# Zero tile and banks first, closer clock-keeping products, an earlier flag and a new order in a fused attention and MLP kernel

## The chip, the cores and the metric

The kernel runs on one core of a Trainium2 chip. Its engines work in parallel, each through its own list of instructions: TensorE (PE, with weight loads as PEld), VectorE (DVE), ScalarE (ACT), GpSimd (POOL) and SyncE (SP, which issues most of the transfers). They wait for each other by semaphores. The metric is the device time of one execution in microseconds (us), from the first instruction to the last and with a little around it; lower is better.

## The reference

The program computes a linear attention with a decaying state and puts its output through a two-layer MLP whose gate is a cosine. r, k, v, w and u are of 4 bytes, w_in and w_out of 8 bytes (the kernel reads each of their numbers as a pair of words).

```
for t in range(S):                       # S = 768, B = 4, H = 8, D = 48
    cur   = (u * k_t) outer v_t
    y_t   = r_t @ (state + cur)
    state = w * state + k_t outer v_t
x = y as (B*S, H*D)                      # 3072 x 384
h = x @ w_in                             # 384 x 2048
out = (h * cos(h)) @ w_out               # 2048 x 384
```

## The kernel before

The 3072 tokens are cut into 24 chunks of 128. A chunk of the attention is computed in matrix form: k and r are multiplied by tables of powers of the decay w (`decT_k`, `decT_r`, `dec_k`, built once at the start from w by a transpose, line 539, and VectorE, lines 544 to 564), then scores (`mm_a`, line 1072, or `mm_az`, 1211 and 1219), a mask, and the output transposed (`mm_x`, line 1110 or 1268), which becomes x as a high and a low part, `xh` and `xl` (lines 1281 and 1286). The first six chunks take an own "early" way with transposes on TensorE (line 946); the others come "late", with VectorE's transposes. Each weight tile is loaded raw, converted by ScalarE, VectorE and GpSimd, and split into a high and a low part (`conv`, lines 740 to 787).

Three chunks make a block of 384 tokens. A step is one block and one slice of 128 hidden columns: nine products of 384 columns give h (line 376), then ScalarE and VectorE in turn make the whole turns (388), the rest (391), the cosine (394), the gate (1390) and its two parts gh and gl (1393, 1396), and nine products of 384 columns (line 383) add to three accumulators. There are 128 steps; the last two work in pieces of 128 columns. Results are copied (1423, 1425) and stored (1435 to 1439).

All this is written as about 2345 operations, each with its engine, a due time, a cost, what it needs, and its buffers. `Plan.order` (line 243 on) goes through a table of numbers, PLACE, which holds each operation's rank: on each engine the operation of lowest rank is next, and the planner works out a start for it from the costs. The program is then emitted in the order of those starts. So PLACE sets each engine's list, and the planned starts set two more things: which buffer an operation gets, and how many clock-keeping products stand in a gap of TensorE. These are products of a tile of zeros, `warm`, into an unused part of bank 2 of the accumulators (`warm_up`, line 1452). They add zero and depend on nothing but the zero tile and on what was read last from that part of the bank; they are there so that TensorE has work in a gap. `start_banks` (line 527) is a group of six products of 512 columns of the same zeros, which sets banks 2 to 7 once.

At the start VectorE clears `warm` (line 496, `start_dve`), the pads of the buffers (line 501, `start_pads`) and a row (508); GpSimd makes the identity; SyncE loads w, then k, r and u. At the end stands a second way through the whole program, for inputs out of range: `check_range` looks at the weights again, `flag_set` at w, `fine_min` takes a minimum over the checks (691 to 693), `fine_t` transposes it (696), `flag_all` writes the flag (699, 700), and each engine then loads the flag from memory (line 1467) and branches (line 1468) over the general path. With ordinary inputs that path is not taken.

Of the kernel before, what the change touches and what calls it, by code (L numbers as in the profile page):

```python
# [154 lines left out]
WARM_TO = 75.0  # L155
# [146 lines left out]
def kernel(  # L302
# [11 lines left out]
    nc = tc.nc  # L314
# [5 lines left out]
    P = 128  # L320
# [76 lines left out]
    with ExitStack() as actx:  # L397
# [107 lines left out]
        def wr():  # L505
# [3 lines left out]
        o_pool = op(POOL, -99, 1.0, start_pool)  # L509
        o_pool2 = op(POOL, -98, 2.75, start_pool2)  # L510
        o_dve = op(DVE, -99, 0.2, start_dve)
        o_pads = op(DVE, -98, 2.3, start_pads)

        o_w = op(
            SP,
# [936 lines left out]
        def warm_up(n):  # L1452
            for _ in range(n):
                nc.tensor.matmul(psum[:, 2, DM : DM + P], warm, warm, start=o_banks not in made, stop=True, skip_group_check=True)
# [150 lines left out]
```

## Time and profile before

| | |
|---|---|
| median of 3 runs | 515.59 us (514.53 to 515.60) |
| profiled execution | 516.15 us, its span 514.4 us |
| TensorE busy | 489.1 us, 95% |
| VectorE busy | 390.8 us, 76% |
| ScalarE, GpSimd busy | 304.4 us, 59%; 198.9 us, 39% |
| mean granted clock of TensorE | 0.985 |
| moved by DMA | 60.92 MB, 118 GB/s over the span |

A busy TensorE is not TensorE at its peak: the ends of pipelined matmuls are modelled, and a product of 384 columns that is listed with 340 ns starts 0.175 us after the one before it when nothing is in the way. The clock is a share of 2.4 GHz; 0.5 is its lower level, 1.2 GHz. A wait is named by the operation that ended it.

### The profile page before, as it was taken

The page shows a single profiled execution, that of the slowest core. Times are in us where ns is not written, and L with a number is a line of the kernel's source. Part 1 is how long each engine was busy: PE and PEld are TensorE (multiplying, and loading weights), DVE is VectorE, ACT ScalarE, POOL GpSimd, SP SyncE. Part 2 cuts the span into 40 slices and gives each one's busy share as a digit, 9 for nine tenths or more (in the row PEclk, how much of TensorE's full clock was granted, in tenths as well). Part 3 has the DMA queues.
Part 4 walks back from the last instruction along what each step waited for, and adds up shares of the span by engine and source line. Part 5 has one row for each costly group of instructions (what it writes and reads, how often), then busy time and mean ns, then how long its engine had stood idle before and what let it go on. Part 6 is the DMA issues. An engine that isn't in the chain of part 4 may idle for free.

```text
span 514.4 us, 13429 instructions
## 1 busy us (share of the span) xinstructions
PE 489.1 (95%) x5207; PEld 464.4 (90%) x5207; DVE 390.8 (76%) x813; ACT 304.4 (59%) x775; POOL 198.9 (39%) x198
## 2 busy tenths in 40 slices
PE   6788899999999999999999999999999999999993
PEld 4667799999898998899999999999999999999992
DVE  6888899998999888967777987885575556564652
ACT  1767587885766655565565665656354565454351
POOL 6846445556597767543171442813110020000000
PEclk9978999999999999999999999999999999999997
DMA  7985558868878778573472557643352222010001
GB/s 137 196 177 122 153 168 195 190 173 171 152 149 154 161 140 171 127 171 117 103 180 65 124 148 156 170 84 100 76 138 63 61 59 81 1 48 0 2 0 53
DMA packets 140086, 60.92 MB, mean 118 GB/s; under 512 B 118205, under 2 KB 135870, under 8 KB 140014
## 3 DMA queue, kind: packets, MB, share of 16 engines
q1 hardware_dynamic: 137070, 55.86, 46.1%
q0 software_dynamic: 2656, 3.74, 4.9%
q8 instruction: 42, 0.69, 0.6%
q10 hardware_dynamic: 288, 0.39, 0.2%
q14 instruction: 30, 0.25, 0.1%
HBM read 51.31 MB, written 8.26 MB: 116 GB/s over the span
## 4 chain that ended last, share of the span: by engine, by line
PE 65%; DVE 6%; ACT 1%; DMA 1%; issue 1%; SPq 0%; POOL 0%; DVEq 0%; ACTq 0%
PE psum L376 29%; PE psum L383 29%; PE psum L1268 3%; PE psum L1211 2%; PE psum L1219 1%; DVE gl L1396 1%; DMA raw<-in_r_dram 1%; DVE psum L1390 1%; DVE T L1238 1%; DVE f L391 1%; DVE psum L1253 0%; ACT gh L1393 0%; DVE T L960 0%; ACT qi L388 0%; ACT f L394 0%
## 5 line engine op out<-in xcount | busy, mean ns | idle before, releaser
L383 PE MATMUL psum<-w_out_hi,gh 128*128 128x384 f32 x384 | 133.4, 347 | 2.7 <-ACT gh L1393 2.0
L376 PE MATMUL psum<-xh,w_in_hi 128*128 128x384 f32 x384 | 130.4, 340 | 1.9 <-DVE gl L1396 1.9
L383 PE MATMUL psum<-w_out_hi,gl 128*128 128x384 f32 x384 | 131.0, 341 | 0.6 <-DVE gl L1396 0.6
L383 PE MATMUL psum<-w_out_lo,gh 128*128 128x384 f32 x384 | 130.0, 339 | 0.0
L376 PE MATMUL psum<-xl,w_in_hi 128*128 128x384 f32 x384 | 129.1, 336 | 0.5 <-DVE xl L1286 0.3
L376 PE MATMUL psum<-xh,w_in_lo 128*128 128x384 f32 x384 | 129.3, 337 | 0.0
L1396 DVE TENSOR_TENSOR gl<-psum,gh 128x384 fp32r<-128x384 f32 (+1 forms) x132 | 71.2, 539 | 46.1 <-ACT gh L1393 44.2
L394 ACT ACTIVATE f<-f 128x384 f32<-128x384 f32 (+1 forms) x132 | 67.4, 514 | 51.2 <-DVE f L391 49.2
L388 ACT ACTIVATE qi<-psum 128x384 int32<-128x384 f32 (+1 forms) x132 | 63.2, 480 | 55.6 <-PE psum L376 50.4
L1393 ACT CAST gh<-psum 128x384 fp32r<-128x384 f32 (+1 forms) x132 | 61.6, 468 | 57.4 <-PE psum L383 34.5
L1390 DVE TENSOR_TENSOR psum<-psum,f 128x384 f32<-128x384 f32 (+1 forms) x132 | 72.0, 548 | 24.7 <-ACT f L394 22.8
L391 DVE SCALAR_TENSOR_TENSOR f<-psum,qi 128x384 f32<-128x384 f32 (+1 forms) x132 | 70.7, 537 | 23.8 <-ACT qi L388 23.0
L1190 POOL TENSOR_TENSOR T<-T,k 48x512 f32<-48x512 f32 x36 | 47.2, 1311 | 99.9 <-issue 35.4
L383 PEld LDWEIGHTS psum<-w_out_hi,gh 128*128 128x128 f32 x384 | 72.5, 189 | 6.6 <-ACT gh L1393 2.8
L376 PEld LDWEIGHTS psum<-xh,w_in_hi 128*128 128x128 f32 x384 | 72.1, 188 | 4.6 <-DVE gl L1396 3.4
L383 PEld LDWEIGHTS psum<-w_out_hi,gl 128*128 128x128 f32 x384 | 72.6, 189 | 2.5 <-DVE gl L1396 2.0
L376 PEld LDWEIGHTS psum<-xl,w_in_hi 128*128 128x128 f32 x384 | 72.2, 188 | 1.1 <-DVE xl L1286 1.1
L383 PEld LDWEIGHTS psum<-w_out_lo,gh 128*128 128x128 f32 x384 | 72.4, 189 | 0.0
L376 PEld LDWEIGHTS psum<-xh,w_in_lo 128*128 128x128 f32 x384 | 72.1, 188 | 0.0
L770 POOL TENSOR_TENSOR f<-f,raw 128x384 int32<-128x384 int32 x32 | 35.0, 1094 | 46.2 <-DVE f L759 20.1
L1176 ACT ACTIVATE T<-ident,a 128x128 f32<-128x128 f32 x144 | 47.1, 394 | 2.8 <-DVE a L1032 2.7
L974 POOL TENSOR_TENSOR f<-f,f 128x384 f32<-128x384 f32 x18 | 18.8, 1047 | 38.8 <-DMA f<-in_r_dram 32.1
(146 smaller groups left out, 633.0 us busy)
## 6 DMA issues: line engine op xcount, KB each, us to landing
raw<-in_moe_w_out_dram SPq DMA_DIRECT2D x32, 384.0 KB, 3.7
raw<-in_moe_w_in_dram SPq DMA_DIRECT2D x32, 192.0 KB, 3.9
raw<-in_moe_w_in_dram SPq DMA_DIRECT2D x16, 384.0 KB, 3.7
raw<-in_k_dram SPq DMA_DIRECT2D x71, 80.0 KB, 3.1
raw<-in_r_dram SPq DMA_DIRECT2D x71, 80.0 KB, 2.6
out_dram<-f SPq DMA_DIRECT2D x21, 192.0 KB, 2.5
out_dram<-f POOLq DMA_DIRECT2D x19, 192.0 KB, 4.8
f<-in_k_dram SPq DMA_DIRECT2D x18, 192.0 KB, 3.7
```

The lines of the kernel that those rows point to most:

```text
L376: nc.tensor.matmul(ph, a, b_, start=(i == 0), stop=(i == len(mm) - 1))
L383: nc.tensor.matmul(acc, a[:, ts], b_, start=(first and i == 0), stop=(last and i == 2))
L388: nc.scalar.activation(qi, ph, AF.Copy, scale=INV_2PI, bias=0.25)
L391: nc.vector.scalar_tensor_tensor(q, ph, INV_2PI, qi, op0=ALU.mult, op1=ALU.subtract)
L394: nc.scalar.activation(q, q, AF.Sin, scale=TWO_PI, bias=0.5 * math.pi)
L770: lambda: nc.gpsimd.tensor_tensor(ai(), ai(), cn(), op=ALU.add),
L974: nc.gpsimd.tensor_tensor(mb(), rb(), kb(), op=ALU.mult)
L1176: nc.scalar.activation(to, ident2[:, None, :].to_broadcast([P, 2, SUB]), AF.Copy, scale=ab()[:, h : h + 1])
L1190: nc.gpsimd.tensor_tensor(M_(n)[rows], by_head(rT)[rows], b_late[1]()[rows], op=ALU.mult)
L1390: nc.vector.tensor_tensor(g()[:, cs], ph()[:, cs], q()[:, cs], op=ALU.mult)
L1393: nc.scalar.copy(gh()[:, cs], g()[:, cs])
L1396: nc.vector.tensor_tensor(gl()[:, cs], g()[:, cs], f32(gh())[:, cs], op=ALU.subtract)
```

## The change

It has five parts.

- `start_pads` now comes behind `start_dve` in the plan, so that VectorE clears the zero tile first; the bank products `o_banks` come first on TensorE, and the transpose of w, `o_wT`, is put behind them. The clock-keeping products never set a bank any more (`start=False`).
- The number of clock-keeping products in a planned gap is (gap - 0.1) / 0.057 in place of (min(gap, 6) - 0.3) / 0.09.
- The flag's operations must be planned ahead of the products of step NS - 4, where NS = 128.
- Some planner costs change: pads 2.3 to 2.5, banks 2.6 to 2.75, wN 0.3 to 0.34 (and it counts as a user of the port that VectorE shares with GpSimd), cosine 0.52 to 0.525, gate 0.55 to 0.565, gh 0.51 to 0.48.
- PLACE is a new table of 2345 numbers.

```diff
 PLACE = (
-    6, 0, 4, 7, 2, 1, 16, 9, 11, 18, 20, 24, 27, 249, 8, 3, 5, 35, 15, 13, 22, 25, 31, 21, 28, 30, 33, 37, 40, 29, 39,
+    9, 0, 6, 2, 3, 1, 4, 10, 11, 19, 20, 21, 25, 346, 12, 5, 7, 33, 17, 14, 26, 22, 32, 23, 28, 31, 34, 38, 40, 29,
...
-        o_pads = op(DVE, -98, 2.3, start_pads)
+        o_pads = op(DVE, -98, 2.5, start_pads, behind=[o_dve])
...
-        o_banks = op(PE, -300, 2.6, start_banks, [o_dve], [*b_0, b_warm])
+        o_banks = op(PE, -300, 2.75, start_banks, [o_dve], [*b_0, b_warm])
-        o_wT = op(PE, -95, 0.26, lambda: nc.tensor.transpose(...), [o_w, o_wr, o_pool], [b_w, b_row])
+        o_wT = op(PE, -95, 0.26, lambda: nc.tensor.transpose(...), [o_w, o_wr, o_pool], [b_w, b_row], behind=[o_banks])
...
-        o_wN = op(DVE, -20, 0.3, swap_w, [o_pow])
+        o_wN = op(DVE, -20, 0.34, swap_w, [o_pow], port=True)
...
-            oh = op(PE, s, 1.73, h, [*x_ready[n], *w_ready[2 * f]], [ph, *xs], line="h", mode=1)
+            known = [o_fa] if s == NS - 4 else []
+            oh = op(PE, s, 1.73, h, [*x_ready[n], *w_ready[2 * f]], [ph, *xs], line="h", behind=known, mode=1)
...
-                op(DVE, s + 3, 0.46, flag_all, [o_ft], [b_fine])
+                o_fa = op(DVE, s + 3, 0.46, flag_all, [o_ft], [b_fine])
...
         def warm_up(n):
             for _ in range(n):
-                nc.tensor.matmul(psum[:, 2, DM : DM + P], warm, warm, start=o_banks not in made, stop=True, skip_group_check=True)
+                nc.tensor.matmul(psum[:, 2, DM : DM + P], warm, warm, start=False, stop=True, skip_group_check=True)
...
-                if o.eng == PE and 1.5 < o.start < WARM_TO:
-                    warm_up(int((min(o.gap, 6.0) - 0.3) / 0.09))
+                if o.eng == PE and o_banks.end < o.start < WARM_TO:
+                    warm_up(int((o.gap - 0.1) / 0.057))
```

Where it moves instructions is shown by the lists of the engines. First the start. VectorE's list before, from the last pad (`w`, `k` and so on are buffers, `f` a row buffer) to the first step on the powers of w:

```order
L501 MEMSET w_102 128x8x16
L508 MEMSET f_105 4x2x16
L496 MEMSET warm 128x64
L497 MEMSET pq 128x4
L551 TENSOR_SCALAR pq<-psum 128x4 [waits PE_49]
```

and VectorE's list now, from its first operation:

```order
L342 MEMSET tiny 1x1
L496 MEMSET warm 128x64
L497 MEMSET pq 128x4
L501 MEMSET k_77 128x8x16
L501 MEMSET k_78 128x8x16
```

The zero tile and pq moved from behind the 17 pads to before them. TensorE's list before, around the transpose of w (line 539), which stands behind 25 clock-keeping products and ahead of 20 more; the bank products follow only after the first chunk's transposes:

```order
L1454 LDWEIGHTS warm
L1454 MATMUL psum<-warm 128x128
L539 MATMUL psum<-ident,f_105 128x4 [waits DMAHW0_49,Pool_49]
L1454 LDWEIGHTS warm
L1454 MATMUL psum<-warm 128x128
```

and TensorE's list now at the same place:

```order
L529 LDWEIGHTS warm
L529 MATMUL psum<-warm 128x512
L539 MATMUL psum<-ident,f_105 128x4 [waits DMAHW0_49,DVE_49,Pool_49]
L1455 LDWEIGHTS warm
L1455 MATMUL psum<-warm 128x128
```

The six bank products open the list, the transpose follows them, and 27 clock-keeping products come behind it. In the whole program there are 221 of these where 107 stood: between the transpose of w and the first scores 27, 42 and 20, later bursts of 23, 40, 21, 16 and smaller ones.

Second, the bursts that wait. TensorE's list before, behind the first chunk's output products (line 1110) and state (1125), where a burst of 5 waits for VectorE:

```order
L1110 MATMUL psum<-T,v_80 32x128 [waits Activation_49]
L1110 MATMUL psum<-T,v_80 32x128
L1125 MATMUL psum<-v_80,k_77 48x48 x8
L1454 LDWEIGHTS warm
L1454 MATMUL psum<-warm 128x128 [waits DVE_49]
```

and TensorE's list now, behind the third chunk's state and the fourth chunk's transposes, where a burst of 21 does so:

```order
L1125 MATMUL psum<-v_82,k_79 48x48 x8
L946 MATMUL psum<-ident,early_k_88 112x64 [waits DMAHW5_49,DMAHW4_49,Pool_49]
L946 MATMUL psum<-ident,early_k_88 112x64 x7
L946 MATMUL psum<-ident,early_r_97 112x64 [waits DMAHW7_49,DMAHW6_49]
L946 MATMUL psum<-ident,early_r_97 112x64 x7
L1455 LDWEIGHTS warm
L1455 MATMUL psum<-warm 128x128 [waits DVE_49]
```

The third chunk's products now also stand directly behind the second's; a burst of 8 behind the third chunk's scores waits for ScalarE.

Third, the end. VectorE's list before, to the branch; it ends in the flag:

```order
L1396 TENSOR_TENSOR gl_118<-psum,gh_116 128x128 [waits Activation_49]
L1425 COPY f_111<-psum 128x384 [waits PE_49]
L699 TENSOR_REDUCE fine<-psum 1x1 [waits PE_49]
L700 TENSOR_TENSOR flag<-fine 1x1 [waits DVE_49]
L1467 TENSOR_LOAD flag [waits DVE_49]
L1468 COMPARE_AND_BRANCH
```

and VectorE's list now, around the flag, 27 rows ahead of its branch:

```order
L1397 TENSOR_TENSOR gl_117<-psum,gh_115 128x384 [waits Activation_49]
L391 SCALAR_TENSOR_TENSOR f_105<-psum,qi_114 128x384
L1391 TENSOR_TENSOR psum<-psum,f_105 128x384 [waits Activation_49]
L699 TENSOR_REDUCE fine<-psum 1x1 [waits PE_49]
L700 TENSOR_TENSOR flag<-fine 1x1 [waits DVE_49]
L1397 TENSOR_TENSOR gl_118<-psum,gh_116 128x384 [waits Activation_49]
```

The flag moved from behind the last copy into the middle of the last steps; on TensorE its transpose moved from the last place to 99 rows ahead of it. TensorE's last product of line 376 was followed by 36 of line 383 and is now followed by 42. ScalarE's list ends as before in copy, store, copy, store, load of the flag, branch; SyncE's last store comes before its load of the flag in both.

## Rows read from the trace of the kernel before

**Rows 1.** The page: busy time of TensorE with its share, and its clock by slices of 12.9 us.

```profile
PE 489.1 (95%) x5207; PEld 464.4 (90%) x5207; DVE 390.8 (76%) x813; ACT 304.4 (59%) x775; POOL 198.9 (39%) x198
...
PEclk9978999999999999999999999999999999999997
```

**Rows 2.** Busy time by windows of 4 us in the head; columns in the first row.

```profile
core 0: us, PE busy (x) PEld busy (x) DVE busy (x) ACT busy (x) POOL busy (x), PEclk, DMA share, GB/s
...
20.00:24.00 4.00, 2.21 (x49) 1.77 (x37) 3.66 (x7) 4.00 (x14) 3.17 (x4) 1.00 1.02 194
24.00:28.00 4.00, 3.42 (x60) 2.67 (x62) 3.67 (x7) 1.67 (x4) 2.36 (x2) 0.53 0.91 161
28.00:32.00 4.00, 3.48 (x64) 2.74 (x64) 2.36 (x4) 2.25 (x6) 3.34 (x3) 0.62 1.04 261
...
48.00:52.00 4.00, 4.00 (x19) 3.70 (x15) 3.59 (x8) 3.32 (x8) 2.35 (x3) 0.57 0.30 61
```

**Rows 3.** Timeline of TensorE, first 20 us: start us, us, engine, line, operation, tiles, count.

```profile
3.55 2.85 PE L1454 MATMUL psum<-warm 128*128 128x128 bf16 x25 [3.55 <-DVE pq L497]
6.33 0.26 PE L539 MATMUL psum<-ident,f 4*128 4x4 f32 x1
...
12.22 1.16 PE L1072 MATMUL psum<-T 48*128 48x128 f32 x16 [1.34 <-DVE T L1013]
...
13.77 1.57 PE L1454 MATMUL psum<-warm 128*128 128x128 bf16 x25
```

**Rows 4.** Timeline of VectorE, first 36 us; in brackets the idle time before a row.

```profile
0.96 0.45 DVE L501 MEMSET k<- 128x128 f32 x3
...
3.38 0.11 DVE L496 MEMSET warm<- 128x64 uint32 x1
...
10.88 0.69 DVE L1002 TENSOR_TENSOR T<-psum,decT_r 112x512 f32<-112x512 f32 x1
...
31.54 0.69 DVE L1002 TENSOR_TENSOR T<-psum,decT_r 112x512 f32<-112x512 f32 x1 [1.64 <-ACT T L1022]
```

**Rows 5.** Timeline of TensorE, 19 to 38 us; equal work at two clocks; first hidden product.

```profile
19.18 1.08 PE L1110 MATMUL psum<-T,v 128*32 128x128 f32 x32
...
22.55 0.44 PE L1454 MATMUL psum<-warm 128*128 128x128 bf16 x5 [1.79 <-DVE xl L1286]
...
24.01 1.76 PE L1110 MATMUL psum<-T,v 128*32 128x128 f32 x32
...
37.55 0.44 PE L376 MATMUL psum<-xh,w_in_hi 128*128 128x384 f32 x1
```

**Rows 6.** Tile v up to 30 us: its loads, and from issue to landing.

```profile
L855 SPq DMA_DIRECT2D v<-in_v_dram x3: 431/505/582, 13.0 to 19.0; - x3
...
DMA to landing us min/median/max: 5.7/5.9/6.0
```

**Rows 7.** What TensorE waited for, 80 to 500 us: us in total, times, longest.

```profile
PE psum L376 <- DVE gl L1396: 1.9, 3, 1.1
```

**Rows 8.** The chain that ended last, 440 to 450 us: start us, us, what, count.

```profile
443.89 3.70 PE psum L383 x21
```

**Rows 9.** Timeline of all engines, from 505 us.

```profile
505.54 0.45 PE L383 MATMUL psum<-w_out_hi,gh 128*128 128x384 f32 x1 [0.60 <-ACT gh L1393]
...
506.94 0.15 DVE L700 TENSOR_TENSOR flag<-fine 1x1 int32<-1x1 f32 x1
507.03 0.34 ACTq L1435 DMA_DIRECT2D out_dram<-f  x1
```

**Rows 10.** Line 1468, branch on the flag: ns min/median/max, first and last start.

```profile
L1468 SPq EVENT_SEMAPHORE  x8: 17/17/17, 512.2 to 512.7; - x8
...
L1468 ACTq COMPARE_BRANCH  x1: 54/54/54, 508.2 to 508.2; - x1
...
L1468 ACTq EVENT_SEMAPHORE  x1: 17/17/17, 512.4 to 512.4; - x1
```

**Rows 11.** Line 1601, the end of the program.

```profile
L1601 POOLq EVENT_SEMAPHORE  x4: 17/17/17, 513.6 to 514.3; - x4
```

More of the change, by code (lines that the diff above doesn't have):

```diff
@@ L535, in start_banks @@
                 )
-        o_banks = op(PE, -300, 2.6, start_banks, [o_dve], [*b_0, b_warm])
-        o_wT = op(PE, -95, 0.26, lambda: nc.tensor.transpose(b_w()[:, 0:NP], b_row()[0:NP, 0 : 2 * DP], ident[0:NP, 0:NP]), [o_w, o_wr, o_pool], [b_w, b_row])
+        o_banks = op(PE, -300, 2.75, start_banks, [o_dve], [*b_0, b_warm])
+        o_wT = op(PE, -95, 0.26, lambda: nc.tensor.transpose(b_w()[:, 0:NP], b_row()[0:NP, 0 : 2 * DP], ident[0:NP, 0:NP]), [o_w, o_wr, o_pool], [b_w, b_row], behind=[o_banks])
         def mul(dst, a, b_):
@@ L1399 @@
                 o2 = op(DVE, dd + 0.6, took(0.55), f_rest, [o1], [ph, q, qi], line="rest")
-                o4 = op(ACT, dd + 0.8, took(0.52), f_cos, [o2], [q], line="cos")
-                o5 = op(DVE, dd + 1.0, took(0.55), f_gate, [o4], [ph, q], line="gate")
-                o6 = op(ACT, dd + 1.2, took(0.51), f_gh, [o5], [g, gh], line="gh")
+                o4 = op(ACT, dd + 0.8, took(0.525), f_cos, [o2], [q], line="cos")
+                o5 = op(DVE, dd + 1.0, took(0.565), f_gate, [o4], [ph, q], line="gate")
+                o6 = op(ACT, dd + 1.2, took(0.48), f_gh, [o5], [g, gh], line="gh")
                 o7 = op(DVE, dd + 1.4, took(0.55), f_gl, [o6], [g, gh, gl], line="gl")
@@ L1453, in warm_up @@
             for _ in range(n):
-                nc.tensor.matmul(psum[:, 2, DM : DM + P], warm, warm, start=o_banks not in made, stop=True, skip_group_check=True)
+                nc.tensor.matmul(psum[:, 2, DM : DM + P], warm, warm, start=False, stop=True, skip_group_check=True)
         order = plan.order(PLACE)
-        made = set()
         with tc.manual_schedule():
             for o in order:
-                if o.eng == PE and 1.5 < o.start < WARM_TO:
-                    warm_up(int((min(o.gap, 6.0) - 0.3) / 0.09))
+                if o.eng == PE and o_banks.end < o.start < WARM_TO:
+                    warm_up(int((o.gap - 0.1) / 0.057))
                 o.emit()
-                made.add(o)
     ok = nc.values_load(flag, min_val=0, max_val=1)
```

226 rows, old and new, of the table PLACE are left out of this document.

## Prediction, made before the run

> **What bounds the kernel now.** I read the page's busy times first, then TensorE's clock by slices, then its timeline over the first 60 us, then the last 10 us. TensorE is busy for 95% of the span [rows 1], and between 80 and 500 us all its waits of one kind that matters, for gl, add up to 1.9 us in three waits [rows 7]. So the middle is a stream of products that no reordering shortens much, and what can be won stands in the head (0 to 64 us) and in the tail (after 505 us). In the head the reader is to see three things. First, the opening products on the zero tile begin only at 3.55 us, because TensorE waited for VectorE's clearing of that tile and of pq (3.38 us), which stands behind the pads that VectorE clears from 0.96 us on [rows 3, 4]. 25 of them, 0.106 us apart ((2.85 - 0.31)/24, half clock), then stand in front of the transpose of w, which runs at 6.33 us [rows 3]. Second, the granted clock is 0.53 and 0.62 in two windows from 24 to 32 us and 0.57 in one at 48 us [rows 2]; ahead of the first of them TensorE was busy for 2.21 of 4 us, and it had stood for 1.79 us because a clock-keeping product itself waited for xl [rows 2, 5]. Third, DMA is busy for 0.91 to 1.04 of the windows from 20 to 32 us [rows 2]: inputs arrive at the rate of the queues. In the tail the last products wait 0.60 us for gh, the flag is written at 506.94 us, ScalarE branches at 508.2 us, and nothing computes until the program ends at 514.4 us [rows 9 to 11].
>
> **The change, part by part.** The sum goes against the profiled execution, 516.15 us (span 514.4 us and 1.75 around it); that lies 0.56 above the median of the three runs shown, 515.59, and I take the differences over to that median.
>
> *Zero tile and banks first.* The clearing moves to 0.96 us and takes 0.11, and the first product may follow 0.06 after it, as 3.55 follows 3.49: 1.13 us. The six bank products of 512 columns at half clock take four times 0.106 each, 2.56 together, so the transpose of w can run at 3.7 instead of 6.33: 2.6 us earlier [rows 3, 4]. The chain of decay tables behind it, up to the first use at 10.88 [rows 4], moves with it. What of that reaches the end? The first output products of a chunk ran at 19.18 [rows 5]; v, issued at 13.0, lands 5.7 us later, at 18.7 [rows 6]. So at that place all but 0.5 us is swallowed by the load. But VectorE, which was busy for 3.66 of the 4 us from 20 us on [rows 2], starts its queue earlier and has the weights' conversions behind it sooner. Bounds: 0 and -2.6; I take -1.0, nearer to the load.
>
> *Products close together, in planned gaps.* By the order of instructions there are 221 of them after and 107 before. Each costs 0.056 us at full clock ((1.57 - 0.22)/24) and 0.106 at half [rows 3]. 221 at 0.056 are 12.4 us, all inside gaps in which TensorE would wait. What they may buy is the clock. A mean of 0.53 over 4 us is 3.8 us at half clock, 0.62 is 3.0 and 0.57 is 3.4. TensorE was busy for 6.9 of the 8 us from 24 us and all of the 4 from 48 us [rows 2], and loses half of what it works at half clock: (3.8 + 3.0) x 0.86 / 2 = 2.9, and 1.7; 32 products of line 1110, 1.08 us at full clock and 1.76 in the slow stretch, show the size [rows 5]. Together 4.6 us, if all of it lies on the path. Part of it does: VectorE stood 1.64 us before the row at 31.54, for ScalarE's copy of transposes that ran at half clock [rows 4, 5]. Bounds: 0 (the drops come back, since products still wait for a buffer) and -4.6; I take -2.0, near to that stand.
>
> The same edit has a price. In the new order a burst of 8 waits for ScalarE and one of 21 for VectorE (the second is shown above), as the 5 at 22.55 us did [rows 5]. The planner does not know that wait; when it ends, 29 x 0.056 = 1.6 us of products stand in front of real work. And the 27 and 42 at the start run at half clock until it is granted, 0.05 more each. Bounds: 0 and +3.0 (1.6, and 1.4 for 28 at half clock at the start); I take +0.6, since most of the real work behind them waits for VectorE anyway.
>
> *The flag four steps from the end.* It removes a transpose, a reduction and a comparison behind the last products, and lets SyncE, VectorE, TensorE and GpSimd load the flag and branch while products run. ScalarE cannot: its last store is issued at 507.03 and takes 0.34, the flag was there at 507.09, so its load of the flag and its branch at 508.2 stay [rows 9, 10]. From branch to its next instruction ScalarE takes 4.2 us (508.2 to 512.4), and SyncE does its eight waits only from 512.2 on; with those that follow it is done at 513.6, when GpSimd begins the closing handshake [rows 10, 11]. With SyncE early, ScalarE is the last, one step after 512.4: 513.6 - 512.5 = 1.1 us. Bounds: 0 (the end hangs on something else) and -1.1; I take -1.0. What is late next is ScalarE itself. The moved instructions are one product of 128 columns and two operations on a single row, the second of which took 0.15 us [rows 9]; in the middle they cost what they cost at the end, and SyncE's load of w for them goes a few rows earlier in a queue that then holds little but stores. I count 0. The transposing product now waits for VectorE's minimum over the checks, with twelve products queued behind it; if the minimum is late by one of VectorE's operations it costs about half a microsecond, which the range covers.
>
> The Trainium skill ("Runtime: NRT & Kernel Launch", section "Instruction fetch mechanics") says that a taken branch whose target lies outside the small window of fetched instructions stalls until a DMA brings the target. The 4.2 us between ScalarE's two rows agree [rows 10]. By that rule the stall belongs to each engine that branches, so an early flag hides it for SyncE and not for ScalarE; were it paid once for all, the tail would lose 4.2 and the sum would be 508.4 instead of 511.6.
>
> *Order anew.* The last three steps' products now end in 42 products of line 383 with nothing between, where 36 stood: 6 x 0.176 (3.70/21 [rows 8]) = 1.06 us more cover for the chain of ScalarE and VectorE behind the last step. The wait at the end was 0.60 [rows 9]. Bounds: -1.1 and +0.5; I take -0.6. In the middle the plan is another of the same kind. Its waits for gl were 1.9 us [rows 7]; they may go or double, -1.9 to +1.9, and I take 0. The changed costs of four planner entries and the order given to pads and wN emit no instruction of their own.
>
> Sum: -1.0 - 2.0 + 0.6 - 1.0 - 0.6 = -4.0. 516.15 - 4.0 = 512.15 for a profiled run, 511.6 for the median.
>
> **Rivals.**
> The loads hide the head. If everything up to 60 us goes by landings, the start and the clock give nothing and only the two tail terms stay: 515.59 - 1.6 + 0.6 = 514.6 with the price of the bursts, 514.0 without. For it speak the DMA shares near 1 and the load of v; against it that the third v, issued at 19.0, landed by 25.0 [rows 6], while the x of its block was not there before the first hidden product at 37.55 [rows 5], and that VectorE, idle for 1.64 of the 4 us from 28 us, was not waiting for a load [rows 2, 4].
>
> The bursts become the bound, and it gets slower. Place: the first 15 us. All of 27 + 42 + 20 products stand in front of the first score product, which ran at 12.22 [rows 3]. If the clock stays at half through them, TensorE arrives there at 3.7 + 0.3 + 89 x 0.106 + 1.2 (two groups of 0.6) = 14.6, 2.4 late. With the 1.6 of the waiting bursts, no gain of clock or start, and the tail's -1.6: 515.59 + 2.4 + 1.6 - 1.6 = 518.0. It decides once the full clock comes later than about 10 us; half clock for only the first half costs 2.2 less. For it: before, the first products at 3.55 us were still at half clock at 6.3 us [rows 3]. Against it: products now begin 2.4 us earlier.
>
> The Trainium skill ("TensorE: Matmul & The Clock Gate", part 1) says that TensorE starts at half rate, that activity releases it, and that the point varies from run to run. That is this rival's mechanism; the trace shows the half rate at the start (0.106 us) and one release only, so it cannot show the spread.
>
> The flag does not do what it says: the closing waits hang on a landing or another engine, the tail gives only -0.6, and the time is 512.6.
>
> The new order is better than its equal: the bursts cost nothing, the clock gives all 4.6 and the gl waits go: 515.59 - 1.0 - 4.6 - 1.6 - 1.9 = 506.5 at the far end; half-way between that and my forecast, 509.0, is the time of this case.
>
> **How the numbers follow.** Forecast 511.6, chance 0.52; flag without effect 0.12; loads hide the head 0.18; better order 0.09; bursts slower 0.09. A measurement of this kernel tells about 0.2%, 1.0 us, from no change. Faster than that: the forecast, the flag's case and the better order (0.73) and a third of the loads' case, 0.06: 0.79. Within it: the rest of that, 0.12. Slower 0.09. The range reaches down to the better order, 509.0, and up past the loads' case to 515.0; it leaves out the slower case and the far end below.
>
> **What would show it.** The first product on the zero tile near 1.1 us and the transpose of w near 3.7 to 4.0 (start). Granted clock 1.0 from 24 to 32 and from 48 to 52 us, and 32 products of line 1110 in 1.08 us (clock); if one window is still near 0.5 there, that term is halved. The first product of line 376 at 33 to 35 us instead of 37.5 (head). SyncE's eight waits of the branch line begun before 505 us and the closing handshake begun right after ScalarE's, about 1 us earlier against the last store (flag). No wait over 0.2 us in the last 42 products (order). I am wrong if the first line-376 product stands where it did, or if bursts with a wait push the scores behind them later than before.

## The result and the profile after

The kernel after took 507.67 us (median of 4 runs, 506.51 to 508.12); the kernel before, beside it on the same chip, 515.38 (4 runs, 514.53 to 515.6). The ratio is 0.985, its 95% interval 0.9829 to 0.9871. The change made the kernel 7.7 us faster. The forecast was 511.6, a gain of 4.0, and its range ended at 509.0: the direction was right, the size about half, and the time lies below the range. The profiled execution of after took 507.95 us with a span of 506.2, so 8.2 are to be explained between the two traces.

The page of after, first the busy times and then TensorE's clock, beside [rows 1]:

```profile
PE 491.7 (97%) x5321; PEld 466.4 (92%) x5321; DVE 389.6 (77%) x813; ACT 301.9 (60%) x775; POOL 198.2 (39%) x198
...
PEclk9999999999999999999999999999999999999999
```

The four windows of [rows 2], same columns, now of after:

```profile
20.00:24.00 4.00, 3.76 (x96) 3.19 (x95) 3.58 (x8) 2.94 (x8) 3.57 (x4) 1.00 1.15 184
24.00:28.00 4.00, 3.42 (x89) 2.93 (x87) 3.25 (x8) 3.93 (x12) 1.34 (x2) 1.00 1.26 191
28.00:32.00 4.00, 3.16 (x64) 2.80 (x68) 3.78 (x6) 0.80 (x3) 3.30 (x4) 1.00 1.14 237
...
48.00:52.00 4.00, 3.76 (x70) 2.88 (x62) 3.97 (x9) 1.43 (x5) 2.25 (x3) 1.00 0.53 113
```

The granted clock is full in all four; the half-clock stretches of before are gone. TensorE's timeline of after, at the places of [rows 3] and [rows 5]:

```profile
1.11 2.74 PE L529 MATMUL psum<-warm 128*128 128x512 bf16 x6 [1.11 <-DVE warm L496]
3.79 0.26 PE L539 MATMUL psum<-ident,f 4*128 4x4 f32 x1
...
10.92 1.16 PE L1072 MATMUL psum<-T 48*128 48x128 f32 x16
...
18.99 1.08 PE L1110 MATMUL psum<-T,v 128*32 128x128 f32 x32 [0.54 <-ACT raw L740]
...
35.31 0.44 PE L376 MATMUL psum<-xh,w_in_hi 128*128 128x384 f32 x1
```

The start is 2.54 us earlier at the transpose of w (3.79 for 6.33), 1.30 at the first scores, and only 0.19 at the first output products. At the first hidden product the gain is 2.24 (35.31 for 37.55). Further on there is a landmark that both orders reach with the same work done on the hidden products: the first product of the 13th hidden group, the 109th that reads w_in. Before and after, it is the last row of each piece of TensorE's timeline:

```profile
87.81 0.34 PE L383 MATMUL psum<-w_out_lo,gh 128*128 128x384 f32 x1
87.99 0.34 PE L376 MATMUL psum<-xh,w_in_hi 128*128 128x384 f32 x1
```

```profile
80.03 0.34 PE L383 MATMUL psum<-w_out_lo,gh 128*128 128x384 f32 x1
80.20 0.34 PE L376 MATMUL psum<-xh,w_in_hi 128*128 128x384 f32 x1
```

It stands at 87.99 and at 80.20, 7.8 us apart. That is a little too much, since by then before has done 90 products of line 383 and after 87. Counted by the n-th product of both lines together, after leads by 7.1 there, by 4.9 to 7.6 at places in the middle, where the two orders differ, and by 6.1 at the last product of all, which begins at 506.14 and 500.00. From the last product to the end of the span it is 514.4 - 506.14 = 8.3 before and 6.2 after: 2.1 more. 6.1 + 2.1 = 8.2.

What TensorE waited for in the first 64 us (total, times, longest), before:

```profile
PE psum L1454 <- DVE pq L497: 3.5, 1, 3.5
PE psum L1072 <- DVE T L1002: 1.9, 2, 1.1
PE psum L1454 <- DVE xl L1286: 1.8, 1, 1.8
PE psum L1072 <- DVE early_T L1002: 1.6, 1, 1.6
PE psum L383 <- ACT gh L1393: 1.4, 1, 1.4
PE psum L1072 <- DVE T L1013: 1.3, 1, 1.3
```

and after:

```profile
PE psum L1072 <- DVE T L1002: 1.7, 2, 1.1
PE psum L529 <- DVE warm L496: 1.1, 1, 1.1
PE psum L946 <- POOL early_k L984: 0.8, 1, 0.8
PE psum L1110 <- ACT raw L740: 0.5, 1, 0.5
PE psum L1072 <- ACT T L1022: 0.5, 1, 0.5
```

All rows of this view add up to 12.7 us before and 5.4 after. The waits for xl, early_T and gh, 4.8 us together, are gone but for 0.2. Between 80 and 500 us the waits are as in [rows 7]:

```profile
PE psum L376 <- DVE gl L1397: 1.9, 3, 1.3
PE psum L383 <- DVE gl L1397: 1.1, 2, 0.8
```

In the tail, the line of the branch and of the end, beside [rows 10] and [rows 11]; SyncE's eight waits now run from 501.6 to 504.5:

```profile
L1467 SPq EVENT_SEMAPHORE  x8: 17/17/17, 501.6 to 504.5; - x8
L1467 SPq COMPARE_BRANCH  x1: 50/50/50, 486.2 to 486.2; - x1
L1467 PEldq COMPARE_BRANCH  x1: 3402/3402/3402, 500.3 to 500.3; - x1
...
L1467 ACTq COMPARE_BRANCH  x1: 54/54/54, 501.8 to 501.8; - x1
...
L1467 ACTq EVENT_SEMAPHORE  x1: 17/17/17, 504.4 to 504.4; - x1
```

```profile
L1600 POOLq EVENT_SEMAPHORE  x4: 17/17/17, 505.4 to 506.1; - x4
```

### The profile page after: what moved, and what is told of

Same layout as the page of the kernel before. It is cut to its first block, busy times and chain, and to the rows that moved or that the text cites. A ratio compares the mean times of both kernels' runs of the same rounds, so it can differ in the third digit from the quotient of the medians.

```text
span 506.2 us, 13688 instructions
## 1 busy us (share of the span) xinstructions
PE 491.7 (97%) x5321; PEld 466.4 (92%) x5321; DVE 389.6 (77%) x813; ACT 301.9 (60%) x775; POOL 198.2 (39%) x198
## 4 chain that ended last, share of the span: by engine, by line
PE 42%; issue 22%; DVE 18%; DMA 5%; ACT 5%; SPq 4%; POOL 2%; POOLq 0%; DVEq 0%; ACTq 0%
PE psum L376 19%; PE psum L383 19%; DVE f L391 3%; DVE gl L1397 2%; DVE psum L1391 2%; SPq L862 2%; DMA raw<-in_moe_w_in_dram 2%; DVE T L1238 2%; ACT T L1176 2%; PE psum L1211 1%; PE psum L1268 1%; ACT gh L1394 1%; DMA out_dram<-f 1%; DVE f L759 1%; SPq L638 1%
## 5 line engine op out<-in xcount | busy, mean ns | idle before, releaser
L770 POOL TENSOR_TENSOR f<-f,raw 128x384 int32<-128x384 int32 x32 | 36.4, 1138 | 36.1 <-DVE f L759 12.6
L966 POOL TENSOR_TENSOR T<-T,k 112x512 f32<-112x512 f32 x18 | 23.5, 1305 | 36.2 <-DVE T L960 33.7
```

What stands on the lines that cost most here:

```text
L770: lambda: nc.gpsimd.tensor_tensor(ai(), ai(), cn(), op=ALU.add),
L966: nc.gpsimd.tensor_tensor(t, t, b_late[0]()[0:KP], op=ALU.mult)
```

## The experiments

The theories: *clock* (the half-clock stretches that went are the head's gain), *start* (the early zero tile is), *order* (the row in which the engines take the operations of the head is). Each kernel is compared with the kernel before beside it on its own chip; that took 515.35 to 516.66 there, so the ratios are what to compare.

**The head's parts on the old order.** Three kernels, all from before.

```diff
# zero tile alone (b_zero): the ranks of o_dve and o_pads change places
+        place[i], place[j] = min(place[i], place[j]), max(place[i], place[j])
-        order = plan.order(PLACE)
+        order = plan.order(place)
# closer products alone (b_warm)
-                    warm_up(int((min(o.gap, 6.0) - 0.3) / 0.09))
+                    warm_up(int((o.gap - 0.1) / 0.057))
# both (b_zero_warm): both edits
```

> The kernel before with one edit: VectorE clears the zero tile and pq ahead of the pads instead of behind them; no other order, no other count of clock-keeping products (107). Clock theory (the head's 6.3 us come from the half-clock stretches that go): 515 plus or minus 0.6, the granted clock still near 0.5 somewhere from 24 to 32 and 48 to 52 us. Start theory (the head is earlier because the zero tile, and with it the decay tables, come 2.4 us sooner): 512.5 to 513.5. Order theory (the new order of the head does it): 515 plus or minus 0.6, and both other kernels of the head near 515 too.

> The kernel before with one edit: the number of clock-keeping products in a gap, (gap - 0.1)/0.057 instead of (min(gap, 6) - 0.3)/0.09, so 226 of them instead of 107; the zero tile stays behind the pads. Clock theory: the two half-clock stretches go, 510 to 511.5. Price theory (43 products at half clock stand in front of the transpose of w, 18 more by 0.106 us, and bursts wait): no gain or a loss, 515 to 518. Start theory: 515 plus or minus 0.6. Order theory: the drops come back, 514 to 516.

> The kernel before with both edits of the two kernels beside it: zero tile first, 226 clock-keeping products. Clock theory: as with the closer products alone, 510 to 511.5. Start theory: as with the zero tile alone, 512.5 to 513.5. If the two need each other (the early start pays for the longer bursts): 510 here, and each alone less than half of that gain. Order theory: 514 to 516.

Measured: zero tile alone 514.49 us beside 515.35, ratio 0.9978 (0.995 to 1.0007); closer products alone 517.47, 1.0041 (1.0016 to 1.0066), slower; both 515.87, 1.0004 (0.998 to 1.0028). The clock theory falls here, as its own sign appeared and its gain did not. The windows of the kernel with closer products alone, columns as above:

```profile
24.00:28.00 4.00, 2.70 (x60) 2.44 (x59) 4.00 (x6) 2.99 (x10) 3.43 (x4) 1.00 1.24 195
28.00:32.00 4.00, 3.39 (x92) 2.67 (x84) 4.00 (x8) 2.59 (x7) 3.92 (x4) 1.00 1.12 240
48.00:52.00 4.00, 3.33 (x27) 2.90 (x28) 3.54 (x9) 2.77 (x7) 1.44 (x2) 1.00 0.51 103
```

Clock 1.00 in all of them, as in after; VectorE is busy for all of 24 to 32 us. TensorE's landmark in the same trace:

```profile
3.55 4.32 PE L1454 MATMUL psum<-warm 128*128 128x128 bf16 x43 [3.55 <-DVE pq L497]
7.80 0.22 PE L539 MATMUL psum<-ident,f 4*128 4x4 f32 x1
...
38.55 0.44 PE L376 MATMUL psum<-xh,w_in_hi 128*128 128x384 f32 x1
...
87.53 0.33 PE L376 MATMUL psum<-xh,w_in_hi 128*128 128x384 f32 x1
```

43 products stand in front of the transpose of w, which comes 1.5 us later than before, the first hidden product 1.0 later; at the landmark the kernel is level with before (87.53 for 87.99), with no half clock in its head at all. It doesn't stay level: by the n-th product it is 1.3 us behind at 145 us and 4.3 at the last product. So 3.0 us of its loss come long after its last clock-keeping product (61.3 us), and this trace is the slowest of its 11 runs (520.22); why it loses there is open. The zero tile alone puts the first output products at 19.14, where a wait of 0.97 us ends with the landing of v: the load swallows the early start, as forecast.

**Order alone.** The table of before, with the operations planned for the first 64, 24 or 40 us in the order of after; and after with the order of before between 64 and 470 us.

```diff
# h_abb (64), h_cut24, h_cut40: kernel before; no other line changes
-PLACE = (before's ranks)
+PLACE = (operations that after's plan starts before 64 / 24 / 40 us, by after's ranks, then all others by before's)
# h_aba: kernel after
-PLACE = (after's ranks)
+PLACE = (after's ranks up to 64 and from 470 us, before's between)
```

> The kernel before with one edit: its table takes the order of the kernel after for the 338 planned operations of the first 64 us, and keeps its own for all others; clock-keeping products by the old formula (about 110), flag last, middle and end as before. Order theory (the head's gain is the row in which each engine takes its work): 5 to 6.5 below the kernel before, 509 to 510.5. Clock theory (the order only pays with close products in its gaps): under half of that, 512.5 to 515. If neither alone carries it: 511 to 512.5.

> The kernel after with one edit: between 64 and 470 us its table takes the order of the kernel before. If the middle's order is worth nothing, as the forecast has it: 507 to 508.3. If the gain up to 220 us that is given back by 280 us belongs to the middle's order: 506 here if its loss goes, 509 if its gain goes.

> The kernel before; the operations planned for the first 24 us take the order of the kernel after, all others keep their own (old formula for the clock-keeping products, flag last). The same with the first 64 us gave 509.7. If the gain lies in the opening (zero tile, decay tables, first scores ahead of the weights' conversions): 509.5 to 511. If it grows with each stretch of the head: 512 to 514. If it lies after 24 us: 514 to 515.5, no better than the zero tile alone.

> The kernel before; the operations planned for the first 40 us take the order of the kernel after. If the gain lies in the opening: the same as with 24 us, 509.5 to 511. If it grows with each stretch: 510.5 to 512, between the kernels with 24 and 64 us. If it lies after 40 us (the wait for gh at 60 us): 513.5 to 515.

Measured: 64 us 509.69 beside 515.42, ratio 0.9904 (0.9869 to 0.994), 5.7 faster by the medians, 4.9 by the ratio; 40 us 511.69 beside 516.66, 0.9899 (0.9857 to 0.9942), as good; 24 us 518.73 beside 516.66, 1.0045 (1.0019 to 1.0072), slower. The order theory holds: the table's first 40 us, with the old formula and the old end, give the head's gain (the early zero tile is part of that order). Where the cut falls at 24 us the two orders don't fit at the seam, and the opening alone gives nothing (no expectation allowed for that). The middle in before's order: 508.2, 0.9858 (0.9825 to 0.9891), the same as after. Neither a gain nor a loss belongs to the middle as a whole. With the order of the first 64 us the clock stayed full in the head with the old formula too; two windows and TensorE's landmark in that trace (its line numbers are 5 higher):

```profile
24.00:28.00 4.00, 2.79 (x68) 2.30 (x59) 3.29 (x9) 3.52 (x12) 1.64 (x2) 1.00 1.20 196
28.00:32.00 4.00, 2.70 (x65) 2.07 (x63) 3.97 (x8) 1.29 (x3) 3.31 (x3) 1.00 1.23 228
...
79.82 0.34 PE L381 MATMUL psum<-xh,w_in_hi 128*128 128x384 f32 x1
```

By the n-th product this kernel leads the kernel before by 8.2 us at the landmark, and by 6.4 to 6.6 from 106 us of before on, up to the last product. So some of the lead at the landmark is lost again with the old order of the middle too. The planner costs are the old ones here; the new ones are not needed for this gain.

**The clock, from the other side.** After with the old formula, after without any clock-keeping products, before without any.

```diff
# a_oldwarm: kernel after
-                    warm_up(int((o.gap - 0.1) / 0.057))
+                    warm_up(int((min(o.gap, 6.0) - 0.3) / 0.09))
# a_nowarm: kernel after, b_nowarm: kernel before
+                    warm_up(0)
```

> The kernel after with one edit: clock-keeping products by the old formula, 110 instead of 221, in the same gaps. Order theory: 507 to 508.3, whatever the clock does, since VectorE sets the head. Clock theory: a half-clock stretch comes back in the head and costs 2 to 4: 509.7 to 511.7.

> The kernel after with one edit: no clock-keeping products at all; only the six bank products on the zero tile stay. Order theory: the head's products run partly at half clock, beside a busy VectorE, and cost 1 to 2: 508.7 to 509.7. Clock theory: 511 or more. If the 221 products themselves stand in the way: 506.5 to 507.3.

> The kernel before with no clock-keeping products; the bank products stay. If the clock was never on the head's path: within 1 of the kernel before, in spite of longer stretches at half clock. If the old products did hold something: 517 to 519. If they stood in the way: 513 to 514.5.

Measured: old formula 509.12 beside 515.42, ratio 0.9867 (0.9835 to 0.9898); none 508.27, 0.9862 (0.9827 to 0.9897); before without any 514.75 beside 516.54, 0.998 (0.9955 to 1.0005). None can be told from the kernel it comes from. Two windows of after without the products:

```profile
12.00:16.00 4.00, 2.62 (x30) 2.33 (x28) 3.21 (x6) 1.53 (x6) 4.00 (x5) 0.50 1.09 266
...
28.00:32.00 4.00, 2.79 (x30) 2.50 (x32) 2.95 (x6) 0.84 (x3) 3.14 (x3) 0.50 1.20 227
```

In its trace TensorE stands at half clock for 20.5 us of the head, and its landmark comes at 81.44 where after has 80.20. But that lead of after is gone soon: at 109.65 us TensorE stands there for 1.3 us and waits for gl (the longest of the three waits in the row for 80 to 500 us above), where the kernel without the products has no such wait. From 120 us to the last product the two traces are within 0.1 us of each other. The products at half clock take longer, but in this trace the time comes out of waits for VectorE.

One thing spoke against this. The runs of the kernel before differ among themselves, and over 91 of them the time rises by 0.30 us (error 0.03) with each us at half clock, taken from each run's mean clock and span. So two more kernels take the products' own price out of the comparison.

```diff
# b_warm13: kernel before, closer products from 13 us of the plan on
-                    warm_up(int((min(o.gap, 6.0) - 0.3) / 0.09))
+                    warm_up(int((min(o.gap, 6.0) - 0.3) / 0.09) if o.start < 13.0 else int((o.gap - 0.1) / 0.057))
# a_gap: kernel after, three bursts left out
-                    warm_up(int((o.gap - 0.1) / 0.057))
+                    warm_up(0 if 20.0 < o.start < 31.0 else int((o.gap - 0.1) / 0.057))
```

> The kernel before with the closer products only from 13 us of the plan on; ahead of that the old counts (25, 20, 1), so the transpose of w is not delayed. Clock on the path (0.30 us for each us at half clock, as the runs of the kernel before show among themselves, some 6 to 10 us in the head): ratio 0.994 to 0.9965. Clock only a sign of waits: 0.998 to 1.001. Price of bursts also after 13 us: 1.001 or more.

> The kernel after without its three bursts between 20 and 31 us of the plan (8, 21 and 16 products), in gaps where TensorE waits anyway. Clock on the path: a half-clock stretch comes back behind them, on the first hidden products, and costs 1 to 1.7: ratio to the kernel before 0.987 to 0.9885. Clock only a sign: 0.984 to 0.986. If these bursts stand in front of work: under 0.984.

Measured: 516.52 beside 515.68, ratio 1.002 (1.0 to 1.0041), and 508.54, 0.9856 (0.9838 to 0.9873). The first runs its whole head at full clock and gains nothing. The second falls to half clock where it was meant to, right ahead of the first hidden products, and loses nothing that can be told:

```profile
28.00:32.00 4.00, 2.00 (x32) 1.81 (x32) 3.89 (x7) 1.14 (x4) 3.10 (x3) 0.82 1.19 230
32.00:36.00 4.00, 4.00 (x72) 3.21 (x69) 3.13 (x9) 3.25 (x10) 1.38 (x3) 0.75 0.94 162
```

So in these heads a low clock is mostly a sign of waits, not their cause. That is also how I read the 0.30: a run in which TensorE waits longer, for whatever reason, shows more half clock; this was not tested.

**Which engines' rows.** Before, with only some engines' operations of the first 64 us in the order of after.

```diff
# h_dve: VectorE; h_pe: TensorE; h_sp: the loads; h_pda: TensorE, VectorE and ScalarE
-PLACE = (before's ranks)
+PLACE = (on the engines named, after's ranks for what after's plan starts before 64 us; before's for the rest)
```

> The kernel before; in the first 64 us VectorE alone takes its operations in the order of the kernel after; TensorE, ScalarE, GpSimd and the loads keep theirs. VectorE theory (what it puts ahead of the weights' conversions is the head's gain): 510 to 511.5. If the engines' rows only pay together, since TensorE then asks for its tiles in the old order: 513.5 to 516, about the zero tile alone or worse.

> The kernel before; in the first 64 us the loads alone (the queue of SyncE) are issued in the order of the kernel after; all four computing engines keep theirs. Load theory (the head goes by landings, and the new order lands what is used first): 510 to 513. If loads only matter beside the engines' own rows: 514.5 to 516.

> The kernel before; in the first 64 us TensorE alone takes its operations in the order of the kernel after. If TensorE's row is what counts (output products no longer queued behind scores that wait for VectorE): ratio 0.990 to 0.994. If the rows only pay together: 0.997 or more, or slower.

> The kernel before; in the first 64 us TensorE, VectorE and ScalarE take their operations in the order of the kernel after; GpSimd and the loads keep theirs. If the three computing engines together carry the head's gain: 5 to 6 below the kernel before, as with all engines (ratio 0.988 to 0.991). If the loads' order is needed beside them: half of that or less (0.994 or more).

Measured: VectorE alone 515.35 beside 516.66, ratio 0.998 (0.9953 to 1.0006); the loads alone 515.06, 0.9971 (0.9939 to 1.0003); TensorE alone 517.06 beside 516.54, 1.0022 (0.9999 to 1.0044); the three computing engines together 513.6, 0.9943 (0.9919 to 0.9968). All engines gave 0.9904. Neither TensorE's nor VectorE's row carries the gain by itself, nor do the loads; ScalarE and GpSimd were not run alone. Three engines together carry 0.6 of the 1.0%. The rest seems to need the loads (or GpSimd) beside them, but the two intervals overlap.

**The early start inside the new order.**

```diff
# a_pads: kernel after
         def start_dve():
+            for t in R_k + R_v + X_k + X_v + X_r + R_w1[1:]:
+                nc.vector.memset(t.ap[:, :, D:DP], 0.0)
             nc.vector.memset(warm, 0.0)
...
         def start_pads():
-            for t in R_k + R_v + X_k + X_v + X_r + R_w1[1:]:
-                nc.vector.memset(t.ap[:, :, D:DP], 0.0)
+            pass
```

> The kernel after with one edit: VectorE clears the pads ahead of the zero tile and of pq again, in one planned operation; all else, the 221 clock-keeping products too, stays. The banks' products then begin near 3.5 us. Start theory (in the new order the early start is on the path, since VectorE is the busy engine from there): 509 to 510.5. Forecast's term of 1.0: 508.2 to 509. If the load of v hides it: 507.4 to 508.1.

Measured: 508.93 beside 516.54, ratio 0.986 (0.984 to 0.988). By the ratio that is 0.5 us above after, with an interval of some 1.5 to either side when that of after is counted in. In the trace the transpose of w is 2.4 us later than in after (6.18), the first output products 1.7 (20.71), the first hidden product only 0.35 (35.66); from 120 us to the end it is 1.3 by the n-th product, in a trace that is the slowest of its five runs. What the start is worth lies between nothing and 2.0; the runs can't tell closer.

**The flag.**

```diff
# a_late: kernel after; the flag's transpose and comparison get the last ranks
+        place = list(PLACE)
+        for o_, at in ((o_ft, 9001), (o_fa, 9002)):
+            place[plan.ops.index(o_)] = at
-        order = plan.order(PLACE)
+        order = plan.order(place)
-            oh = op(PE, s, 1.73, h, ..., behind=known, mode=1)
+            oh = op(PE, s, 1.73, h, ..., mode=1)
```

> The kernel after with one edit: the transpose and the comparison of the flag go last, as before the change. Fetch theory (with the flag early SyncE's fetch of its branch target runs under products, and the closing waits begin with the last store's landing): the tail is 1.8 us longer again, 509.2 to 509.9. Forecast on record (ScalarE's own fetch is late next, so 1.1): 508.6 to 509.2. Landing theory (the last store's landing sets the end in any case): 507.4 to 508.2.

Measured: 509.57 beside 515.35, ratio 0.99 (0.9853 to 0.9946). That is 1.9 above after by the medians and 2.6 by the ratios, with an interval of 2.7 to either side, so the runs alone hardly tell it from nothing. Its line of the branch:

```profile
L1470 SPq EVENT_SEMAPHORE  x8: 17/17/17, 505.6 to 506.1; - x8
...
L1470 SPq COMPARE_BRANCH  x1: 50/50/50, 502.1 to 502.1; - x1
```

SyncE branches at 502.1 and does its eight waits only from 505.6 on, 3.5 us later. In after it branched at 486.2, under products; its first wait stands at 501.6, and the next, on the landing of ScalarE's last store, ends at 504.07 (that store was issued at 500.88). After's waits of SyncE that follow those of the branch line:

```profile
L1600 SPq EVENT_SEMAPHORE  x14: 17/28/28, 504.6 to 506.1; - x14
```

From the issue of ScalarE's last store to the end of the span it is 6.7 us here, 5.3 in after and 7.4 before (514.4 - 507.03). All the traces of this document tell more than these three: it is 5.3 to 6.3 in the six with the early flag (mean 5.8) and 6.6 to 7.4 in the fourteen with the flag last (mean 7.0). So the early flag is worth some 1.2 us; before and after happen to lie at the far ends, which is why their tails differ by 2.1. It isn't worth more, since SyncE then waits for the landing of the last store, and that comes later when the flag is early: 3.2 to 4.2 us after its issue in the six, 2.2 to 2.4 in the fourteen. Why was not tested.

## Why the prediction was wrong

**Start, -1.0.** The mechanism was right, the size within what can be told: -1.1 on the old order (0.9978, though its interval just reaches no change), some 0.5 in the new. On the old order the load of v hides it at the first output products, as forecast.

**Clock, -2.0: this step failed.** The forecast's sign was met, clock 1.0 in all the windows that it named, and 32 products of line 1110 in 1.08. But I took the lengthening of TensorE's work at half clock for time on the path. The row that I had beside it said otherwise: TensorE stood in the same windows and waited for xl, scores and ScalarE, and slower products only fill such a wait. Without one clock-keeping product the kernel before is no slower, and the kernel after, at half clock for 20.5 us, some 0.6, less than its runs can tell. At full clock in its whole head the kernel before gains nothing either (1.002, 1.0 to 1.0041; the forecast's -2.0 would be 0.996). The rule of the Trainium skill ("TensorE: Matmul & The Clock Gate", part 1), that activity releases the half rate, agrees with these traces: the clock came back wherever the products stood closer. What the full rate is worth in these heads is next to nothing.

**Bursts, +0.6.** On the old order they cost more: closer products alone +2.1, and +1.4 when added to the early zero tile (0.9978 to 1.0004, with intervals that overlap). 43 of them stand there in front of the transpose of w, which I had bounded for the new order only. That this is what costs is not shown: most of the loss in the trace comes behind 145 us, and with the old counts ahead of 13 us the closer products still gain nothing. In the new order, where the bank products come first and bursts stand in longer gaps, leaving them out changes nothing that can be told; the rival "bursts slower" did not come true, and what it names may hold for the old order.

**The order, 0 in the middle and -0.6 at the end, none in the head: this step failed too, and here the gain was.** I gave the new order terms for the middle and for the end and none for the head, which I had filled with the start and the clock. The head's order alone is 5.7 us by the medians (4.9 by the ratio, 3.1 to 6.8), with whatever the early zero tile in it is worth. For the middle 0 was right (0.9858 with the old order there, 0.985 with the new). At the end the waits that the sum removed did go: the largest wait in the last products is 0.25 us, and the end is 0.5 better than the middle left it (by the n-th product, the lead is 5.6 where the last 36 of before begin and 6.1 at the last one). That term was right. The bound that I gave, -1.9 to +1.9 for a plan "of the same kind", came from the waits of 80 to 500 us [rows 7]; the waits of the first 64 us, 12.7 in the same view, were never set against the new order.

**Flag, -1.0: near in size, but the step behind it failed.** I had ScalarE's branch as next in line and SyncE's waits as done. What is late next is the landing of the last store and then SyncE itself: 19 waits one after another, 0.067 us apart, from 504.07 to 505.27, beside which ScalarE, through at 504.4, does not count. And of the four engines that were to branch while products run only SyncE does so: in after TensorE and VectorE branch at 500.3, behind the start of the last product, and GpSimd at 501.2. The early flag gives some 1.2 in the traces, so that the term of 1.0 fits is partly luck. The rival that let the closing waits hang on a landing named the right thing, but with no gain from the flag. The rule of the Trainium skill ("Runtime: NRT & Kernel Launch", section "Instruction fetch mechanics"), that a taken branch out of the fetched window stalls until its target is fetched, agrees: SyncE's 3.5 us are no longer waited for when it branches early, and ScalarE, which branches late, still takes 2.5.

The sum of what the runs and traces show: 5.7 (head's order, the start within it) + 0.5 (end) + 1.2 (flag) = 7.4, against 7.7 measured; with 4.9 by the ratio for the head it is 6.6. Both fit the interval of the measurement (6.6 to 8.8), which is no proof that nothing is missing. The range was too narrow below: its far end, 506.5, was built mostly from the clock, the range stopped half-way to it, and no case held an order that shortens the head. That this far end lies near the measured time is luck, since neither the 4.6 of the clock nor the 1.9 of the waits for gl in it came (those waits are 1.9 in after too).

## What to carry to other kernels

Where several engines hand work to each other, a lower clock on one of them is a cost only if it is the one waited for; read its waits in the same window before counting its slowness, and take the clock away (or give it) in an experiment before paying for it. When an order is computed anew, add up the waits of the stretch with the most of them and let the forecast reach as far as their sum; a row that is changed on one engine alone tells little about the whole order. For a program's end, look for the engine that does its closing waits last and for the last transfer that it waits for, and move that engine's branch ahead of it; here that gave some 1.2 us.

## What was not expected of the hardware

The time from a branch to the engine's next instruction is not a fixed one. ScalarE took 4.2 us before [rows 10], 2.5 in after and 3.7 with the flag late; over all the traces of this document 3.5 to 4.2 with the flag last (14 traces) and 2.5 to 3.1 with the early flag (6). The earlier branch of SyncE may have left the others less to share; no run was made on it. TensorE does not follow this: it took 0.5 us before (507.73 to 508.24), 3.5 in after (500.31 to 503.77) and 4.6 with the flag late (501.81 to 506.38), and over all traces either 0.4 to 0.6 or 3.4 to 4.6, with both in either group. What decides there is open.

The slower run of an order cut at 24 us (0.45% above before, where either whole order is better) shows that one head's order can't be joined to another's at every place. Which hand-over of the first 40 us is worth most stays open: the waits for xl, early_T and gh shrank or went together with the whole order, and no run changed one of them alone.
